# Attention and two mixtures of experts on one core: staggered first blocks, a catch-up after them, and new figures for the host-side scheduler

## The chip, the cores and the metric

One core of a Trainium2 chip runs the whole program in one launch. The metric is the device time of an execution in microseconds, as the median of several runs. Five engines work side by side, each through its own list of instructions in the order in which the program wrote them: TensorE (PE in the rows, its weight loads PEld), VectorE (DVE), ScalarE (ACT), GpSimd (POOL), and SyncE (SP), which here only issues transfers.

## The reference, cut to what matters

```python
def phi(x):                                   # q, k: 4 x 8 x 576 x 64, w_phi: 64 x 128
    proj = np.einsum('bhsd,df->bhsf', x, w_phi)
    proj = proj - np.max(np.abs(proj), axis=-1, keepdims=True)
    return np.concatenate([np.exp(proj), np.exp(-proj)], axis=-1)
q_p, k_p = phi(q), phi(k)
kv = np.einsum('bhsf,bhsd->bhfd', k_p, v)
z = np.sum(k_p, axis=2)
attn = np.einsum('bhsf,bhfd->bhsd', q_p, kv) / (np.einsum('bhsf,bhf->bhs', q_p, z)[..., None] + 1e-06)
x = attn.transpose(0, 2, 1, 3).reshape(2304, 512)
h = x @ moe_w_in                              # 512 x 2048, held as 64-bit floats
x = (h - np.tanh(h)) @ moe_w_out              # 2048 x 512: "first MoE"
p = probs / (probs.sum(-1, keepdims=True) + 1e-09)
out = sum(p[:, e:e + 1] * (np.maximum(x @ w1[e], 0) @ w2[e]) for e in range(4))   # "second MoE"
```

## The kernel before

**Stages.** The attention turns 2304 tokens into x, in 8 blocks of 288 tokens. The first MoE has a hidden width of 2048, cut into 16 chunks of 128. The weights of 8 chunks fit into SBUF at a time (the tiles `wslot`), so the first MoE goes over all tokens twice: in the first pass block j of 288 tokens goes through chunks 0 to 7 as soon as its x exists, while the attention of block j+1 runs between; in the second pass 6 blocks of 384 tokens go through chunks 8 to 15 ("late" in the code), and the two partial sums are added. Then comes the second MoE, which the change doesn't touch.

**Attention.** `k_task(b, p, t0)` makes the features of two heads of k and their product with v (16 of them; 4 ahead of block 0, two more in each of blocks 0 to 5). `q_task(b, s, p, t0)` makes two heads of q for one block (4 a block): transposes, a projection in three matmuls (high and low halves of the operands), copies `pq` and exponentials `ea` and `eb` by ScalarE, a row maximum by VectorE (`qm`, L585), twelve products with `kv` for each of `ea` and `eb` (L598), the division, and a transpose back into `xmem`, which holds x as a high and a low part for two blocks at a time (ring `xt_r`). When a block is done, x is also stored in DRAM (`xs`), for the second pass.

**One visit of a chunk** by a block is `moe_slot` and `moe_x2`. Layer 1 is 12 matmuls of 288 columns (L373, `bank<-xmem,wslot`). Then h - tanh(h) is made: ScalarE squares and takes tanh (L651, L652), VectorE does L653, L654, L655 and the predicated copy L657, ScalarE L656 and the high part `ghm` (L658), and GpSimd or VectorE the low part `glm` (L248 or L247, by the lists `GL` and `GL2`). Layer 2 is 12 matmuls into the four accumulators (`acc`), held back by `LAG = 3` visits. After a block's last visit `evac` copies the accumulators out by ScalarE (L715) and stores them in DRAM (`x2s`).

**Weights.** A chunk has two parts (w_in and w_out). `to_f32` loads one as 64-bit words and makes 32-bit floats by one ScalarE, one GpSimd (L321) and three VectorE instructions (L322, L323, L324); `split_w` makes the high part by ScalarE (L329) and the low part by GpSimd (L330). `direct` does that for chunks 0 to 7. `park` makes the floats of chunks 8 to 15 during blocks 3 to 6 and stores them in DRAM; `staged` loads and splits them when the slots come free, around the start of the second pass.

**Order.** The order of every engine's list comes from a simulation on the host before the launch. `add` puts a piece of work (a node) with an engine, a modelled duration, the nodes it needs and a due time into a graph; `Issue.run` plays the graph through, and each time that an engine falls idle it emits the ready node with the lowest due time. A due time is only a priority: a node that is ready early goes early. `HOP` is the modelled time from the end of a node to a node that waits for it; `c_act`, `c_dve`, `c_pool` and `c_pe` are modelled durations by width. On the chip the order is fixed, and each instruction waits for what it needs. `T_START`, `T_BLK`, `LEAD`, `W_LEAD` and `T_TASK` place the due times: block j's at 50 + 44 j us.

Of the kernel before, what the change touches and what calls it, by code (L numbers as in the profile page):

```python
# [40 lines left out]
class Node:  # L41
    __slots__ = ("eng", "dur", "busy", "fn", "need", "after", "at", "key", "banks", "frees", "home")
# [29 lines left out]
class Issue:  # L72
# [3 lines left out]
    HOP = {"PE": 0.28, "ACT": 0.16, "DVE": 0.16, "POOL": 0.22, "SP": 0.1}  # L76
# [26 lines left out]
    def run(self):  # L103
        ready = {e: [] for e in self.HOP}
        idle = dict.fromkeys(self.HOP, True)
        back = False
        events, n, now = [], 0, 0.0
# [10 lines left out]
        while events:  # L118
# [11 lines left out]
            for e, r in ready.items():  # L130
# [8 lines left out]
                if r:  # L139
# [43 lines left out]
def c_pe(n):  # L183
    return max(n * 0.000417 + 0.013, 0.112)
# [3 lines left out]
def attention_moe_moe_kernel(  # L188
# [122 lines left out]
    def to_f32(c, part, due, early=0.0):  # L311
# [99 lines left out]
    def k_task(b, p, t0):  # L411
# [38 lines left out]
        pd = add("PE", 1.05, proj, [a1], t0 + 1.2, [kT, *kds], banks=pb)  # L450
        for e in range(2):
            bk, kd, kp, due = pb[e], kds[e], kp_r.take(), t0 + 2 + e
# [3 lines left out]
            x1 = add("ACT", c_act(512), lambda kd=kd, kp=kp: ACT.activation(out=kp.t[:, :, 0, :], in_=kd.t, func=ACTF.Exp), [a], due + 1, [kd, kp])  # L456
            x2 = add("ACT", c_act(512), lambda kd=kd, kp=kp: ACT.activation(out=kp.t[:, :, 1, :], in_=kd.t, func=ACTF.Exp, scale=-1.0), [a], due + 1, [kd, kp])
# [19 lines left out]
        for e in range(2 if b else 0):  # L477
# [53 lines left out]
    def q_task(b, s, p, t0):  # L531
# [28 lines left out]
        for e in range(2):  # L560
# [305 lines left out]
    for i in range(2):  # L866
        lx_r.turns.append(xt_r.turns[i - 2])
# [235 lines left out]
```

## Time and profile before

| | |
|---|---|
| median of 3 runs | 1439.3 us |
| lowest and highest | 1436.97 and 1439.79 us |
| profiled execution, its own time | 1439.52 us |
| its span, first to last instruction | 1436.8 us |
| PE busy | 1398.9 us, 97% |
| DVE, ACT, POOL busy | 1067.8, 663.6, 670.8 us |
| mean granted TensorE clock | 0.994 |

The views cover the span; 2.7 us of the execution's own time lie outside it. Ends of matmuls are modelled and matmuls overlap, so PE's busy share is a rough upper bound of its work. The granted clock is a share of full speed (1.00 is 2.4 GHz, half of it 1.2 GHz).

### The profile page before, as it was taken

What the parts mean: (1) busy time and instruction counts of PE and PEld (TensorE: products, weight loads), DVE (VectorE), ACT (ScalarE), POOL (GpSimd) and SP (SyncE); (2) the same over time, 40 slices, a digit from 0 to 9 for tenths busy, and PEclk for the clock granted to TensorE, in tenths of its full rate; (3) what the DMA queues carried; (4) which work ended last, traced back from release to release, by engine and by line L of the source; (5) the groups of instructions that cost most, each with busy time, mean ns of one, the idle gap of its engine ahead of it and who ended that gap; (6) DMA issues with size and microseconds to landing.
All of it is one profiled execution on the core that took longest, in us unless ns stands there. A gap on an engine that the chain in (4) does not pass through costs nothing.

```text
span 1436.8 us, 23312 instructions
## 1 busy us (share of the span) xinstructions
PE 1398.9 (97%) x8704; PEld 1274.5 (89%) x8704; DVE 1067.8 (74%) x1871; ACT 663.6 (46%) x1575; POOL 670.8 (47%) x551
## 2 busy tenths in 40 slices
PE   8988999999999999999899999999999999999998
PEld 6777888989999899998799999898999989999997
DVE  5898578888867867556787777877777787777774
ACT  6756566666656545444433333433333343333331
POOL 2786354554413326213544544654454466445441
PEclk9999999999999999999999999999999999999999
DMA  6532235443416413212212212233122123221211
GB/s 175 166 112 58 83 88 152 131 131 105 136 56 202 120 45 104 62 34 69 85 60 74 68 65 73 68 110 103 65 68 74 59 74 109 67 73 60 74 44 44
DMA packets 128704, 127.43 MB, mean 89 GB/s; under 512 B 53968, under 2 KB 104272, under 8 KB 128592
## 3 DMA queue, kind: packets, MB, share of 16 engines
q1 hardware_dynamic: 128432, 125.89, 28.4%
q8 instruction: 68, 1.11, 0.3%
q14 instruction: 44, 0.36, 0.1%
q10 hardware_dynamic: 160, 0.07, 0.0%
HBM read 101.29 MB, written 24.64 MB: 88 GB/s over the span
## 4 chain that ended last, share of the span: by engine, by line
PE 83%; DVE 8%; ACT 3%; POOL 2%; issue 2%; DMA 1%; SPq 1%; ACTq 0%; DVEq 0%; POOLq 0%
PE acc L373 36%; PE bank L373 35%; PE bank L598 3%; DVE hsm L655 2%; PE bank L498 1%; PE bank L582 1%; DVE thm L657 1%; PE bank L556 1%; DVE glm L247 1%; PE acc L498 1%; PE bank L448 1%; PE acc L508 1%; DVE thm L654 1%; ACT sqm L656 1%; DVE hsm L653 1%
## 5 line engine op out<-in xcount | busy, mean ns | idle before, releaser
L1034 ACT ACTIVATE h<-xc 128x384 fp32r<-128x384 f32 x160 | 84.1, 525 | 426.7 <-DVE xc L1038 426.7
L923 POOL TENSOR_TENSOR wslot<-wtmp,wslot 128x512 fp32r<-128x512 f32 x96 | 124.2, 1294 | 274.2 <-ACT wslot L921 171.6
L373 PE MATMUL acc<-ghm,wslot 128*128 128x288 f32 (+1 forms) x896 | 234.8, 323 | 7.9 <-ACT ghm L658 4.7
L373 PE MATMUL bank<-xmem,wslot 128*128 128x288 f32 (+1 forms) x1224 | 218.3, 314 | 1.8 <-ACT kv L528 1.6
L373 PEld LDWEIGHTS bank<-xmem,wslot 128*128 128x128 f32 x1224 | 187.5, 189 | 3.5 <-ACT kv L528 1.8
L373 PE MATMUL acc<-wslot,h 128*128 128x512 f32 x768 | 188.3, 392 | 0.0
L1010 POOL TENSOR_TENSOR wslot<-raw,wslot 128x512 fp32r<-128x512 f32 x96 | 138.0, 1457 | 100.8 <-ACT wslot L1010 100.8
L1035 DVE SCALAR_TENSOR_TENSOR h<-xc,h 128x384 fp32r<-128x384 f32 x160 | 103.2, 645 | 94.7 <-ACT h L1034 94.7
L373 PEld LDWEIGHTS acc<-ghm,wslot 128*128 128x128 f32 x896 | 159.9, 190 | 14.0 <-ACT ghm L658 5.5
L373 PE MATMUL bank<-wslot,h 128*128 128x512 f32 x672 | 168.2, 395 | 1.5 <-ACT h L1034 1.5
L373 PEld LDWEIGHTS acc<-wslot,h 128*128 128x128 f32 x768 | 143.2, 188 | 27.7
L248 POOL TENSOR_TENSOR glm<-thm,ghm 128x288 fp32r<-128x288 f32 (+1 forms) x76 | 72.9, 960 | 179.3 <-ACT ghm L658 161.5
L373 PEld LDWEIGHTS bank<-wslot,h 128*128 128x128 f32 x672 | 126.0, 189 | 27.1 <-ACT h L1034 2.3
L373 PE MATMUL acc<-glm,wslot 128*128 128x288 f32 (+1 forms) x448 | 141.3, 315 | 3.4 <-POOL glm L248 2.6
L923 POOL TENSOR_TENSOR wslot<-raw,wslot 128x512 fp32r<-128x512 f32 x96 | 108.7, 1152 | 15.6 <-ACT wslot L921 15.6
L657 DVE COPY_PREDICATED thm<-sqm,hsm 128x288 f32<-128x288 int32 (+1 forms) x112 | 77.2, 690 | 43.4 <-ACT sqm L656 43.0
L656 ACT ACTIVATE sqm<-sqm,b_m 128x288 f32<-128x288 f32 (+1 forms) x112 | 64.3, 574 | 87.6 <-DVE hsm L655 85.3
L1038 DVE TENSOR_TENSOR xc<-bank,xc 128x384 f32<-128x384 f32 x168 | 92.3, 550 | 12.1 <-PE bank L373 12.0
L1038 DVE TENSOR_TENSOR xc<-acc,xc 128x384 f32<-128x384 f32 x168 | 92.2, 550 | 11.2 <-PE acc L373 10.9
L919 DVE TENSOR_TENSOR wtmp<-raw 128x256 f32<-128x256 f32 x96 | 98.4, 1026 | 0.0
L653 DVE SCALAR_TENSOR_TENSOR hsm<-bank,sqm 128x288 f32<-128x288 f32 (+1 forms) x110 | 54.6, 496 | 52.3 <-ACT thm L652 51.5
L373 PEld LDWEIGHTS acc<-glm,wslot 128*128 128x128 f32 x448 | 85.2, 190 | 4.8 <-POOL glm L248 3.2
(267 smaller groups left out, 3181.7 us busy)
## 6 DMA issues: line engine op xcount, KB each, us to landing
raw<-in_moe_w_dram SPq DMA_DIRECT2D x96, 512.0 KB, 3.5
xs<-xmem SPq DMA_DIRECT2D x16, 576.0 KB, 4.2
raw<-in_moe_w_in_dram SPq DMA_DIRECT2D x16, 512.0 KB, 4.6
raw<-in_moe_w_out_dram SPq DMA_DIRECT2D x16, 512.0 KB, 5.2
qraw<-in_q_dram SPq DMA_DIRECT2D x32, 144.0 KB, 2.9
x2s<-x2m SPq DMA_DIRECT2D x8, 576.0 KB, 3.4
out_dram<-yacc SPq DMA_DIRECT2D x18, 256.0 KB, 2.1
kraw<-in_k_dram SPq DMA_DIRECT2D x16, 256.0 KB, 3.6
```

What stands on the lines that cost most here:

```text
L248: return add("POOL", c_pool(n), lambda: POOL.tensor_tensor(out=o, in0=a, in1=b, op=op), deps, due, bufs)
L373: PE.matmul(ps, lhsT=a, rhs=b, start=start and n == 1, stop=stop and n == 3 * len(pairs))
L598: PE.matmul(side(ab)[:, e, r], lhsT=x.t[:, e, r * QP:(r + 1) * QP], rhs=kv.t[:, e, ab], start=True, stop=True)
L653: y1 = add("DVE", c_dve(N), lambda: DVE.scalar_tensor_tensor(out=hs.t, in0=at(bk)[:, 0:N], scalar=P1, in1=sq.t, op0=ALU.mult, op1=ALU.mult ...
L656: x3 = add("ACT", c_act(N, ptr=True), lambda: ACT.activation(out=sq.t, in_=sq.t, func=ACTF.Relu, scale=-1.0, bias=b_m[:, 0:1]), [y3], due ...
L657: y4 = add("DVE", c_dve(N), lambda: DVE.copy_predicated(out=th.t, mask=sq.t.bitcast(I32), data=hs.t), [x3, y2, y3], due + 1.4, [th, sq, hs])
L919: steps = [("DVE", 0.36, lambda o=o, a=a, b=b, op=op: DVE.tensor_tensor(out=o, in0=a, in1=b, op=op)) for o, a, b, op in sums]
L923: steps.append(("POOL", c_pool(n), lambda h=h, l=l, src=src: POOL.tensor_tensor(out=l, in0=src, in1=f32(h), op=ALU.subtract)))
L1010: todo2 = [lambda c=c: (ACT.activation(out=vh[:, c], in_=r2[:, c], func=ACTF.Copy), POOL.tensor_tensor(out=vl[:, c], in0=r2[:, c], in1=f32 ...
L1034: ACT.activation(out=hh, in_=src, func=ACTF.Relu)
L1035: DVE.scalar_tensor_tensor(out=hl, in0=src, scalar=0.0, in1=f32(hh), op0=ALU.max, op1=ALU.subtract)
L1038: DVE.tensor_tensor(out=o, in0=bk, in1=a, op=ALU.add)
```

## The change

The first pass no longer takes all 8 chunks through every block: block 0 visits chunks 0 and 1, block 1 chunks 0 to 3, block 2 chunks 0 to 5, and blocks 3 to 7 all eight (`FIRST`). After block 7, three catch-up blocks make the missing 6, 4 and 2 visits: each loads its x again from `xs` into the ring `xt_r` and ends with `add_x2` in place of `evac`, which loads the stored partial sum, adds the four accumulators to it on VectorE and stores it again. Chunk c is asked for by the first block that visits it (`need`). The second pass starts with the ring where the catch-up left it.

The scheduler's model is replaced: durations by width, hops, a drain at the end of a node, a switch time on TensorE when a node has another tile shape (`mode`), and one shared `port` for every GpSimd node and the marked VectorE nodes, which the simulation runs one after the other. Due times get new constants. In `q_task` the exponentials read the copy `pq` in SBUF, two instructions of 2 x 288 columns, instead of the two PSUM banks, four of 288; the 24 products with `kv` become two nodes of 12, one for `ea` and one for `eb`. The projection itself is as it was.

The diff, cut: the scaling of due times inside `k_task` and `q_task` by `K_PACE` and `Q_PACE`, the marks `mode` and `port` on single nodes, and the durations written into single nodes (those of the weights' conversion among them) are left out.

```diff
-T_START = 50.0
+T_START = 44.3
 LEAD = 26.0
-T_BLK = 44.0
-K_LEAD = 0.0
+T_ATT = 22.0
+T_SLOT = 3.3
+T_X2 = 14.8
+K_PACE = 0.78
+Q_PACE = 0.96
+PARK_LEAD = -8.8
+FIRST = (2, 4, 6)
+K_LEAD = -0.4
 GL = ["POOL"]
 GL2 = ["DVE", "POOL"]
-W_LEAD = 5.0
-T_TASK = 8.0
+W_LEAD = 10.5
+T_TASK = 7.7
...
-    HOP = {"PE": 0.28, "ACT": 0.16, "DVE": 0.16, "POOL": 0.22, "SP": 0.1}
+    HOP = {"PE": 0.055, "ACT": 0.037, "DVE": 0.033, "POOL": 0.08, "SP": 0.1}
+    DRAIN = {"PE": 0.16, "ACT": 0.11, "DVE": 0.082, "POOL": 0.035, "SP": 0.0}
+    SWITCH = 0.2
...
-                    event(now + x.busy, "idle", e)
-                    end = now + x.dur
+                    start = now
+                    if x.port:
+                        start = max(now, port)
+                    if e == "PE" and x.mode != mode:
+                        start, mode = now + self.SWITCH, x.mode
+                    event(start + x.busy, "idle", e)
+                    end = start + x.dur + self.DRAIN[e]
+                    if x.port:
+                        port = start + x.busy
...
 def c_act(n, psum=False, ptr=False):
-    return n / 1200.0 + (0.05 if psum else 0.093) + (0.093 if ptr else 0.0)
+    return n * 0.00091 + 0.03 if psum else n * 0.00081 + (0.205 if ptr else 0.105)
 def c_dve(n, fast=False):
-    return n / 960.0 + 0.09
+    return n / 960.0 + 0.066
 def c_pool(n):
-    return n * 0.00225 + 0.22
+    return n * 0.00228 + 0.1
...
-            def exps(e=e):
-                for x, sg in ((ea, 1.0), (eb, -1.0)):
-                    xe.append(add("ACT", c_act(N, True), lambda x=x, sg=sg: ACT.activation(out=x.t[:, e], in_=at(pb[e])[:, 0:N], func=ACTF.Exp, scale=sg), [a], t0 + 2.4, [x], frees=[pb[e]]))
+        xe = [add("ACT", c_act(2 * N), lambda x=x, sg=sg: ACT.activation(out=x.t, in_=pq.t, func=ACTF.Exp, scale=sg), pc, t0 + Q_PACE * 2.4, [pq, x]) for x, sg in ((ea, 1.0), (eb, -1.0))]
...
-        a = add("PE", 2.05, mm, [*xe, s2, *kvdone], t0 + 5, [ea, eb, kv, u], banks=nb)
+        pm = [add("PE", 1.02, lambda ab=ab, x=x: mm(ab, x), [xe[ab], *([] if ab else [s2]), *kvdone], t0 + Q_PACE * 5 + 0.5 * ab, [x, kv, u], bank=nb[ab]) for ab, x in enumerate((ea, eb))]
...
-    t_blk = [T_START + j * T_BLK for j in range(NBLK + 1)]
+    n_first = [FIRST[j] if j < len(FIRST) else NC1 for j in range(NBLK)]
+    t_len = [(T_ATT if j + 1 < NBLK else 0.0) + T_SLOT * n_first[j] for j in range(NBLK)]
+    t_blk = [T_START + sum(t_len[:j]) for j in range(NBLK + 1)]
+    need = [min(j for j in range(NBLK) if n_first[j] > c) for c in range(NC1)]
...
     for c in range(NC1):
-        wdone[c] = direct(c, c, t_blk[0] + W_LEAD * (c - 1))
+        j = need[c]
+        wdone[c] = direct(c, c, t_blk[j] + t_len[j] / n_first[j] * c - W_LEAD * 2)
...
+    def add_x2(j, due):
+        def fn(ends):
+            xb = x2p_r.take()
+            ld = dma([(xb.t, x2s[j])], [x2_done[j]], due - 12, [xb])
+            done = []
+            for i in range(KD):
+                a = add("DVE", c_dve(N), lambda i=i: DVE.tensor_tensor(out=xb.t[:, i, :], in0=accs[i][:, 0:N], in1=xb.t[:, i, :], op=ALU.add), [ends[i], ld], due, [xb])
+                acc_users[i].append(a)
+                done.append(a)
+            x2_done[j] = dma([(x2s[j], xb.t)], done, due + 1, [xb])
+        return fn
...
-        moe_block(j, [(c, c) for c in range(NC1)], xt, xdone, t_blk[j], T_BLK / NC1, GL if j < 4 else GL2 if j < NBLK - 1 else ["DVE"], evac, s_rings, N, LAG)
+        moe_block(j, [(c, c) for c in range(n_first[j])], xt, xdone, t_blk[j], t_len[j] / n_first[j], GL if j < 4 else GL2 if j < NBLK - 1 else ["DVE"], evac, s_rings, N, LAG)
...
-    t2, dt = t_blk[NBLK - 1] + 24, 4.2
+    t2 = t_blk[NBLK]
+    for j in range(len(FIRST)):
+        rest = [(c, c) for c in range(n_first[j], NC1)]
+        xt = xt_r.take()
+        ld = dma([(f32(xt.t[i]), xs[j][i]) for i in range(2)], [xs_done[j]], t2 - 10, [xt])
+        moe_block(j, rest, xt, [ld], t2, T_SLOT, ["DVE", "POOL"], add_x2, s_rings, N, LAG)
+        t2 += T_SLOT * len(rest)
```

## Rows read from the trace of the kernel before

**Rows 1.** The page's first line: the span.

```profile
span 1436.8 us, 23312 instructions
...
```

**Rows 2.** Stretches: length; PE, PEld, DVE, ACT, POOL busy (count); clock; DMA share; GB/s.

```profile
...
0.00:40.00 40.00, 35.49 (x312) 27.82 (x314) 24.48 (x64) 25.04 (x67) 11.50 (x13) 0.96 0.68 173
40.00:60.00 20.00, 19.45 (x199) 15.86 (x195) 14.94 (x32) 13.87 (x40) 13.84 (x10) 1.00 0.55 157
60.00:140.00 80.00, 67.67 (x552) 59.33 (x551) 73.76 (x135) 51.43 (x141) 61.94 (x52) 0.96 0.34 102
140.00:200.00 60.00, 59.67 (x539) 53.11 (x538) 39.00 (x86) 36.98 (x109) 28.74 (x33) 1.00 0.26 75
200.00:420.00 220.00, 217.57 (x1906) 198.67 (x1904) 175.66 (x383) 140.98 (x408) 101.06 (x95) 1.00 0.38 118
420.00:455.00 35.00, 35.00 (x267) 35.00 (x266) 23.56 (x48) 19.84 (x50) 8.86 (x8) 1.00 0.57 173
455.00:480.00 25.00, 21.74 (x129) 20.91 (x129) 22.97 (x33) 18.35 (x43) 15.77 (x11) 0.95 0.59 174
...
655.00:700.00 45.00, 37.91 (x200) 34.35 (x200) 29.50 (x48) 17.99 (x39) 16.29 (x13) 1.00 0.27 88
...
```

**Rows 3.** The same view, the first 20 us of the third stretch.

```profile
...
60.00:80.00 20.00, 18.79 (x186) 16.08 (x184) 18.88 (x41) 14.54 (x43) 15.99 (x15) 1.00 0.51 155
...
```

**Rows 4.** The chain that ended last, from 60 to 140 us, by line.

```profile
...
by line: issue 13.7%; PE bank L373 9.0%; POOL wtmp L321 6.5%; POOL glm L248 6.5%; DVE thm L657 4.8%; POOL wslot L330 4.7%; DVE hsm L655 4.6%; DVE kd L455 4.0%; PE acc L373 3.6%; DVE km L454 3.1%; POOL xf L608 2.9%; POOL ks L485 2.8%; ACT kp
...
```

**Rows 5.** Groups of VectorE instructions from 60 to 140 us: busy, mean ns, idle before.

```profile
...
L324 DVE SCALAR_TENSOR_TENSOR wtmp<-raw,wtmp 128x512 uint32<-128x512 uint32 x10 | 9.8, 993 | 0.0
L655 DVE SCALAR_TENSOR_TENSOR hsm<-sqm,hsm 128x288 f32<-128x288 f32 x10 | 9.3, 928 | 0.0
...
L657 DVE COPY_PREDICATED thm<-sqm,hsm 128x288 f32<-128x288 int32 x10 | 8.1, 824 | 0.3 <-ACT sqm L656 0.3
...
```

**Rows 6.** Groups of VectorE instructions from 200 to 420 us, same columns.

```profile
...
L657 DVE COPY_PREDICATED thm<-sqm,hsm 128x288 f32<-128x288 int32 x35 | 21.2, 606 | 7.6 <-ACT sqm L656 7.2
L655 DVE SCALAR_TENSOR_TENSOR hsm<-sqm,hsm 128x288 f32<-128x288 f32 x34 | 20.1, 591 | 0.0
L585 DVE TENSOR_REDUCE qm<-bank 96x3 f32<-96x384 f32 x36 | 19.0, 548 | 11.9 <-PE bank L582 9.2 <-ACT eb L566 2.4 <-ACT x2m L715 0.2
L653 DVE SCALAR_TENSOR_TENSOR hsm<-bank,sqm 128x288 f32<-128x288 f32 x34 | 15.4, 452 | 11.5 <-ACT thm L652 10.9
L654 DVE TENSOR_TENSOR thm<-bank,thm 128x288 f32<-128x288 f32 x34 | 15.2, 446 | 0.0
L323 DVE SCALAR_TENSOR_TENSOR wtmp<-raw,wtmp 128x512 uint32<-128x512 uint32 x16 | 14.3, 895 | 0.2
L324 DVE SCALAR_TENSOR_TENSOR wtmp<-raw,wtmp 128x512 uint32<-128x512 uint32 x16 | 14.0, 877 | 0.0
...
L322 DVE TENSOR_SCALAR wtmp<-wtmp 128x512 uint32<-128x512 uint32 x16 | 9.0, 565 | 4.2 <-POOL wtmp L321 4.2
...
L454 DVE TENSOR_REDUCE km<-bank 128x4 f32<-128x512 f32 x12 | 7.7, 682 | 1.6 <-PE bank L448 1.6
...
```

**Rows 7.** VectorE in order of time, 440 to 482 us: start, length, instruction.

```profile
...
441.08 0.45 DVE L655 SCALAR_TENSOR_TENSOR hsm<-sqm,hsm 128x288 f32<-128x288 f32 x1
...
444.25 1.40 DVE L655 SCALAR_TENSOR_TENSOR hsm<-sqm,hsm 128x288 f32<-128x288 f32 x1
...
```

**Rows 8.** GpSimd in order of time, 440 to 480 us, same columns.

```profile
...
444.05 2.77 POOL L330 TENSOR_TENSOR wslot<-raw,wslot 128x512 fp32r<-128x512 f32 x2 [9.24 <-ACT wslot L329]
...
```

**Rows 9.** Waits from 440 to 500 us: in total, times, longest.

```profile
...
PE acc L373 <- ACT x2m L715: 3.2, 1, 3.2
...
```

**Rows 10.** DMA issues by transfer: count, KB each, median us from issue to landing.

```profile
...
xmem<-xs SPq DMA_DIRECT2D x4, 576.0 KB, 4.3
...
```

**Rows 11.** Groups of ScalarE instructions from 140 to 440 us: busy, mean ns, idle before.

```profile
...
L566 ACT ACTIVATE eb<-bank 128x288 f32<-128x288 f32 x44 | 19.6, 445 | 0.0
...
L456 ACT ACTIVATE kp<-kd 128x512 f32<-128x512 f32 x18 | 11.3, 629 | 6.5 <-DVE kd L455 5.2 <-POOL wtmp L321 1.2
...
```

More of the change, by code (lines that the diff above doesn't have):

```diff
@@ L41 @@
 class Node:
-    __slots__ = ("eng", "dur", "busy", "fn", "need", "after", "at", "key", "banks", "frees", "home")
+    __slots__ = ("eng", "dur", "busy", "fn", "need", "after", "at", "key", "banks", "frees", "home", "mode", "port")
 class Bank:
@@ L81, in __init__, with add @@
         self.free_lent, self.n_lent = list(range(banks, banks + lent)), lent
-    def add(self, eng, dur, fn, deps=(), due=0.0, bufs=(), bank=None, banks=(), frees=(), busy=None, early=0.0, home=False):
+    def add(self, eng, dur, fn, deps=(), due=0.0, bufs=(), bank=None, banks=(), frees=(), busy=None, early=0.0, home=False, mode="all", port=False):
         x = Node()
-        x.home = home
+        x.home, x.mode, x.port = home, mode, port or eng == "POOL"
         x.eng, x.dur, x.busy, x.fn, x.banks, x.key = eng, dur, busy or dur, fn, [bank] if bank else list(banks), (due, len(self.nodes))
@@ L106, in run @@
         back = False
+        mode, port = "all", 0.0
         events, n, now = [], 0, 0.0
@@ L246, in tt @@
         if eng == "DVE":
-            return add("DVE", c_dve(n), lambda: DVE.tensor_tensor(out=o, in0=a, in1=b, op=op), deps, due, bufs)
+            return add("DVE", c_dve(n), lambda: DVE.tensor_tensor(out=o, in0=a, in1=b, op=op), deps, due, bufs, port=True)
         return add("POOL", c_pool(n), lambda: POOL.tensor_tensor(out=o, in0=a, in1=b, op=op), deps, due, bufs)
@@ L448, in proj @@
                     PE.matmul(at(pb[e])[:, j * 128:(j + 1) * 128], lhsT=kT.t[h0:h0 + 64, j * 128:(j + 1) * 128], rhs=wphi[h0:h0 + 64, :], start=True, stop=True)
-        pd = add("PE", 1.05, proj, [a1], t0 + 1.2, [kT, *kds], banks=pb)
+        pd = add("PE", 0.9, proj, [a1], t0 + K_PACE * 1.2, [kT, *kds], banks=pb, mode="rows")
         for e in range(2):
-            bk, kd, kp, due = pb[e], kds[e], kp_r.take(), t0 + 2 + e
+            bk, kd, kp, due = pb[e], kds[e], kp_r.take(), t0 + K_PACE * (2 + e)
             m = km.t[:, 4 * e:4 * e + 4]
@@ L625, in to_p @@
             return t[:, p, :].rearrange("d (p r) -> d p r", r=3)
-        a = add("ACT", c_act(N, True), lambda: ACT.activation(out=to_p(xh), in_=from_r(), func=ACTF.Copy), [a], due + 2.5, [xt], frees=[ob])
+        a = add("ACT", c_act(N, True), lambda: ACT.activation(out=to_p(xh), in_=from_r(), func=ACTF.Copy), [a], due + Q_PACE * 2.5, [xt], frees=[ob])
         done.append(a)
-        a = add("DVE", c_dve(N), lambda: DVE.tensor_tensor(out=to_p(xl), in0=from_r(), in1=to_p(f32(xh)), op=ALU.subtract), [a], due + 3, [xt], frees=[ob])
+        a = add("DVE", c_dve(N), lambda: DVE.tensor_tensor(out=to_p(xl), in0=from_r(), in1=to_p(f32(xh)), op=ALU.subtract), [a], due + Q_PACE * 3, [xt], frees=[ob])
         done.append(a)
         if p == NP - 1:
-            xs_done[j] = dma([(xs[j][i], f32(xt.t[i])) for i in range(2)], done, due + 3, [xt])
+            xs_done[j] = dma([(xs[j][i], f32(xt.t[i])) for i in range(2)], done, due + Q_PACE * 3, [xt])
         n_att[0] += 1
@@ L828, in fn @@
             def fn(order, s=s, c=c, gg=gg, first=first, last=last, due=due):
-                ends = moe_x2(s, wdone[c], gg, first, last, due + lag * dt, order, n)
+                ends = moe_x2(s, wdone[c], gg, first, last, due + T_X2, order, n)
                 if last:
-                    end(j, due + lag * dt + 1)(ends)
+                    end(j, due + T_X2 + 1)(ends)
                 return ends
@@ L863, in x_again @@
                 SP.dma_start(out=f32(t)[:, :, o:o + m], in_=src[:, k0:k0 + n, a:a + m])
-    lx_r = Ring([lambda i=i: late_xt(i) for i in range(2)])
-    for i in range(2):
-        lx_r.turns.append(xt_r.turns[i - 2])
+    xt_first = len(xt_r.turns) % 2
+    lx_r = Ring([lambda i=i: late_xt((i + xt_first) % 2) for i in range(2)])
+    lx_r.turns.extend(xt_r.turns[-2:])
     l_rings = []
```

109 lines of the change are left out of this document (52 added, 57 removed).

## The prediction

> **What bounds the kernel now.** I read the span cut into stretches first, then the chain of waits in the worst stretch, then the groups of VectorE instructions there and in a good stretch. The change leaves alone everything after the second pass of the first MoE, and there PE hardly stops. PE's lost time lies earlier. I count as lost the time without a matmul, plus length times (1 - clock) where the granted clock's mean is under 1.00. From 0 to 60 us that is 4.5 + 0.6 idle and 0.04 x 40 = 1.6 of clock, 6.7 us. From 60 to 140 us it is 80 - 67.67 = 12.3 idle and 0.04 x 80 = 3.2 of clock: 15.5 us, the largest sum. From 140 to 200 it is 0.3, from 200 to 420 2.4, from 455 to 480 3.3 + 0.05 x 25 = 4.5, from 655 to 700 7.1 [rows 2]. So the pass that the change rebuilds holds some 29 us to be had at the very most, 2% of a span of 1436.8 us [rows 1].
>
> In the worst stretch VectorE is busy 73.76 of 80 us (92%) and GpSimd 61.94 (77%); from 200 to 420 us they are at 80% and 46% [rows 2]. The chain there runs through both of them and matmuls are a small part of it [rows 4]. The reader sees why in the counts: ten of the 16 weight parts that the first visits need (L324 x10) and ten visits (L655 x10) fall into these 80 us [rows 5]. Block 0 asks for all eight chunks' weights at once, and PE has no other work ready.
>
> **Prices.** A visit on PE is 24 of the 267 matmuls that fill 35 us [rows 2], 3.15 us. From 200 to 420 us there are 34 visits (L655), 18 q tasks (two L585 each) and 6 k tasks (two L454 each) [rows 6]; PE's 217.57 us less 34 x 3.15 leave 110.5 us, 4.6 a task, so 27.6 for a block's six tasks. On VectorE a visit is 0.606 + 0.591 + 0.452 + 0.446 = 2.10 us, a part 0.895 + 0.877 + 0.565 = 2.34 us [rows 6]; the remainder of 175.66 - 71.9 - 37.3, less some 6 us of smaller groups, is 60 us or 2.5 a task, 15 a block. In the worst stretch the visit's L655 and L657 are 0.34 and 0.22 us dearer and the part's L324 0.12 [rows 5, 6]: 2.65 a visit, and 2.45 a part.
>
> **The first blocks.** Before, block 0 with the ten parts costs VectorE 15 + 8 x 2.65 + 10 x 2.45 = 60.7 us against 27.6 + 8 x 3.15 = 52.8 on PE: VectorE is the bound by 8 us, and waits on chains make it 15.5. After, I spread these ten parts over blocks 0 to 2 as 4, 4 and 2, though due times are only priorities. VectorE then has 15 + 5.3 + 9.8 = 30.1 us beside 33.9 on PE, 15 + 10.6 + 9.8 = 35.4 beside 40.2, and 15 + 15.9 + 4.9 = 35.8 beside 46.5: 89, 88 and 77%. I don't believe the third, as the parts slip, and take 88% for it too. What PE loses at such a share I interpolate: 1.1% at 80% (2.4 of 220 us [rows 2]) and 6.0% at 94% (60 to 80 us: 1.21 of 20 [rows 3]), so 4% at 88 or 89%: 4.8 us over the 120.6 us. The term is -15.5 - 0.3 + 4.8 = -11 us. Its ends are -15.8 (no loss left) and 0: at the whole worst stretch's rate, 15.5 in 80 us at 92%, 120 us would lose 23 us and nothing is won.
>
> The Trainium skill, "Perfetto Trace Analysis", section "Identifying the Most-Contended Engine", says that the share of matmul time is a poor measure of TensorE and that weight-load time is a better one. By it the worst stretch has 59.33 of 80 us of weight loads, 74%, against 90.3% from 200 to 420 us [rows 2], which is 12.9 us of loads missing, or 14.3 us of time; the term would be -9.8 instead of -11. The trace agrees with the rule in kind, and I keep my count.
>
> **The catch-up.** The 12 visits move; PE's 12 x 3.15 = 37.8 us stay the same and now stand where no attention runs. There VectorE is at 23.56 of 35 us [rows 2], 2.1 us a visit by its share. Added are 12 additions of an accumulator to SBUF, priced by L654, which also has one operand in each memory: 0.446 us [rows 6], 5.4 us, so 2.1 + 0.45 = 2.6 us beside 3.15 on PE, 81%: hidden but for about 1% of 37.8 us, and if the cover is gone, 5.4 us. The loads of x (two per block, 4.3 us to landing [rows 10]) are covered by 6 and 4 visits for the first two blocks. The second pass's first load must wait until the second catch-up block has left its buffer; PE then has two layers 1 and three layers 2 left, 5 x 1.6 = 8 us, against 4.3 to 8.6 us for one transfer or two in turn: 0 to 1 us. The 6 loads of x, 3 loads and 3 stores of sums also pass SP's queue among the parked weights; its transfers keep the DMA engines 38 to 59% busy here [rows 2]. I take +1 us, between 0 and +18 (below).
>
> **The scheduler's figures** change the order everywhere ahead of the second MoE, and the trace of before can't show the new order. What they can win lies in the losses outside the worst stretch: 6.7 us from 0 to 60, 2.4 from 200 to 420, and 4.5 from 455 to 480, 13.6 us; the wait for transfers in the first 20 us stays. What they can lose is not bounded by a row; I take the same size as the nearest comparable, 4.5 us, for another bad stretch. I choose -2.5, nearer to nothing than to the gain.
>
> **The query tasks.** Four exponentials from PSUM at 0.445 us become two from SBUF of 576 columns, 0.71 us each by L456's 0.629 for 512 [rows 11]: 1.78 us become 1.42 per task on ScalarE, which is 64% busy [rows 2]. The first twelve products wait for one exponential less. Other tasks and visits hide both; with no cover it would be at most the 2.4 us counted above. The split of the 24 products adds no matmul. All this: 0.
>
> **Sum.** -11 + 1 - 2.5 = -12.5 us from the profiled execution's own 1439.5 (2.7 over its span), 0.2 above the median of the runs, so 1426.8 against 1439.3: I predict 1427 us. A change under 0.2% (2.9 us) can't be told from none.
>
> **Rivals.** *More is won*: the new figures fit well enough that the first blocks lose only 1.1%, as from 200 to 420 us (1.3 us), and two thirds of the other 13.6 us go too: -14.5 - 9 + 1 = -22.5, 1417 us. For it: L655 and L657 take 0.93 and 0.82 us in the worst stretch and 0.59 and 0.61 in the good one [rows 5, 6], and the old model has one duration for each; against: some of the 6.7 us at the start is waiting for transfers.
>
> *It doesn't do what it says*: the same parts and tasks ahead of block 3 keep VectorE and GpSimd at 92%, and the loss only spreads. The first term is 0 to -3, the rest as above: 1438 us. For it: the part work isn't less, it only comes later; against: PE now has other blocks' attention to run meanwhile.
>
> *The catch-up becomes VectorE's and GpSimd's* (slower). The second pass's weights are split by GpSimd just there; beside two such splits, 2.77 us [rows 8], L655 took 1.40 us instead of 0.45 [rows 7]. With 0.95 more on each visit, VectorE needs 2.6 + 0.95 = 3.55 us against 3.15: 12 x 0.4 = 4.8 us behind. Each of three more block ends then hands the accumulators over late, as PE waited 3.2 us for L715 once [rows 9]: 9.6 us; and the late load adds up to 4. That is 18 us, net of the gains of -13.5 a time of 1444 us. It decides once the catch-up loses over 16 us. The Trainium skill, "SBUF — State Buffer", section "Who interferes with whom", states that a VectorE instruction with two SBUF operands and a GpSimd one that reads SBUF shut each other out for a whole instruction; by that rule L655 and L657 of every catch-up visit beside a split are held, as the rows on L655 agree, while the additions are not.
>
> **Chances and range.** Forecast 0.54 (own range 1420 to 1433), more won 0.22, not what it says 0.12, slower 0.12. Faster by over 0.2%: the first two and a sixth of the third, 0.78; same 0.1; slower 0.12. The range 1411 to 1441 reaches from the second's better end to the foot of the fourth.
>
> **What would show it.** Right: from 60 to 140 us PE idle under 6 us with the clock at 1.00, VectorE under 92%; the second pass beginning some 12 us earlier than before's 455; no wait of over 2 us on the accumulators between the catch-up blocks. Wrong: VectorE over 95% in the catch-up, PE waiting on additions or on `xmem`, or the loss found again between 140 and 300 us. What would break the forecast most is the order itself, which no row shows.

## The result, and the profile after

The changed kernel takes 1421.4 us (median of four runs, 1418.5 to 1425.1) beside 1438.6 for the kernel before on the same chip: a ratio of 0.9883 with an interval of 0.9855 to 0.991. That is 5.6 us below the forecast of 1427, in the range and in the forecast's own range of 1420 to 1433, but 4.4 us above the rival "more is won" (1417), so nearer to that as a time; as a change, -17.1 us lies between the -12.5 of the one and the -22.5 of the other. The profiled execution took 1419.9 us. Its span:

```profile
span 1417.9 us, 23306 instructions
...
```

The matmuls are the same 8704 in both. The stretches of the span, up to 200 us as in [rows 2] and from there cut 15 to 20 us earlier, to stand at the same work (columns as there):

```profile
...
0.00:40.00 40.00, 34.35 (x295) 27.41 (x295) 24.78 (x60) 25.30 (x59) 15.29 (x17) 0.96 0.70 187
40.00:60.00 20.00, 19.72 (x202) 15.30 (x203) 19.26 (x38) 16.41 (x44) 11.40 (x10) 1.00 0.51 147
60.00:140.00 80.00, 76.84 (x720) 66.47 (x719) 68.70 (x144) 55.71 (x148) 59.64 (x53) 0.98 0.42 122
140.00:200.00 60.00, 56.45 (x496) 50.19 (x496) 47.56 (x99) 37.72 (x100) 36.30 (x37) 0.97 0.41 129
200.00:400.00 200.00, 197.53 (x1695) 182.47 (x1692) 157.93 (x349) 128.05 (x340) 80.05 (x77) 1.00 0.37 119
400.00:440.00 40.00, 40.00 (x303) 40.00 (x303) 30.02 (x61) 25.44 (x63) 14.66 (x12) 1.00 0.46 157
440.00:465.00 25.00, 25.00 (x171) 25.00 (x171) 21.79 (x40) 16.15 (x36) 11.70 (x9) 1.00 0.82 269
465.00:640.00 175.00, 175.00 (x1011) 174.91 (x1010) 126.78 (x216) 87.41 (x179) 52.13 (x43) 1.00 0.25 74
640.00:680.00 40.00, 34.93 (x192) 32.76 (x190) 26.61 (x41) 15.50 (x32) 17.08 (x13) 1.00 0.28 87
...
```

Lost time, counted as in the prediction:

| part of the work (before / after) | before | after |
|---|---|---|
| start, 0 to 60 us | 6.7 | 7.5 |
| first blocks, 60 to 140 | 15.5 | 4.8 |
| 140 to 200 | 0.3 | 5.3 |
| 200 to 420 / 200 to 400 | 2.4 | 2.5 |
| handover to the second pass, 420 to 480 / 400 to 465 | 4.5 | 0 |
| second pass, 480 to 655 / 465 to 640 | 1.7 | 0 |
| its end, 655 to 700 / 640 to 680 | 7.1 | 5.1 |
| sum | 38.2 | 25.2 |

So 13.0 of the 18.9 us by which the span is shorter are lost time that is gone, against a forecast of 12.5. The other 5.9 us are nearly all busy time of the same matmuls (1398.9 to 1392.3 us, 6.6 less, of which the table has counted 1.1 as clock), and the prediction left them out. Where they lie is seen at equal work, by the start of the n-th matmul in each trace (the stretches above are cut by time, and count less):

| up to matmul | after is ahead by, us | won since the line above | by the table above |
|---|---|---|---|
| 3800, the second pass has begun | 6.7 | 6.7 | 4.8 |
| 3900, behind the stall at the handover | 12.0 | 5.3 | 4.5 |
| 4500, in the second pass | 13.9 | 1.9 | 1.7 |
| 5200, behind its end | 17.0 | 3.1 | 2.0 |
| the last | 19.1 | 2.1 | not counted |

So all but the last line is won where lost time is won too. The 2.1 us of the last line come in the second MoE, which the change leaves alone: the granted clock is 0.91 from 980 to 1000 us before and 1.00 from 960 to 980 us after, at about the same work. In e7 below nothing is won there (17.6 us ahead at matmul 5200, 17.4 at the end), so I put these 2.1 us down to the execution and not to the change.

In the worst stretch the chain of waits now runs mostly through PE itself, where [rows 4] had GpSimd's L321 and L248 near its head:

```profile
...
by line: PE bank L600 15.4%; PE acc L389 10.5%; PE bank L514 8.9%; PE acc L600 5.2%; PE bank L389 4.2%; PE bank L572 3.8%; DVE wtmp L339 3.5%; DVE wtmp L340 3.3%; PE bank L585 2.9%; PE acc L514 2.9%; PE bank L464 2.9%; issue 2.6%; PE bank L
...
```

The groups of VectorE instructions there, to hold against [rows 5] (L340 was L324, L657 was L655, L659 was L657; busy, mean ns, idle before):

```profile
...
L340 DVE SCALAR_TENSOR_TENSOR wtmp<-raw,wtmp 128x512 uint32<-128x512 uint32 x8 | 6.9, 867 | 0.0
...
L657 DVE SCALAR_TENSOR_TENSOR hsm<-sqm,hsm 128x288 f32<-128x288 f32 x5 | 3.1, 612 | 0.0
L659 DVE COPY_PREDICATED thm<-sqm,hsm 128x288 f32<-128x288 int32 x5 | 2.8, 553 | 0.0
...
```

Ten visits have become five and ten parts eight, and a visit's two long instructions are a third shorter (928 and 824 ns before). PE filled the time with other blocks' attention: its count rose from 552 to 720. But 140 to 200 us, nearly full before, now loses 5.3 us with VectorE at 79%, not 65%. Over both stretches 5.7 us are saved, not 11.

These stretches are cut by time, not by work. The start of the second pass is in keeping with them: its first product comes 5.6 us ahead of before's 455 (PE in order of time):

```profile
...
449.40 1.41 PE L389 MATMUL bank<-xmem,wslot 128*128 128x384 f32 x7
...
```

### The profile page after: what moved, and what is told of

It reads as the page before. It is cut to its first block, busy times and chain, and to the rows that moved or that the text cites. A ratio compares the mean times of both kernels' runs of the same rounds, so it can differ in the third digit from the quotient of the medians.

```text
span 1417.9 us, 23306 instructions
## 1 busy us (share of the span) xinstructions
PE 1392.3 (98%) x8704; PEld 1272.5 (90%) x8704; DVE 1075.4 (76%) x1889; ACT 664.9 (47%) x1511; POOL 660.9 (47%) x545
## 4 chain that ended last, share of the span: by engine, by line
PE 90%; DVE 5%; ACT 2%; DMA 2%; issue 1%; SPq 0%; POOL 0%; ACTq 0%; DVEq 0%
PE acc L389 39%; PE bank L389 38%; PE bank L600 3%; PE bank L514 2%; PE bank L585 1%; PE bank L572 1%; PE acc L600 1%; DVE hsm L657 1%; PE bank L464 1%; DVE xc L1063 1%; PE acc L514 0%; DMA raw<-in_moe_w_out_dram 0%; DMA xq<-x2f 0%; PE bank L528 0%; PE bank L615 0%
## 5 line engine op out<-in xcount | busy, mean ns | idle before, releaser
L389 PE MATMUL acc<-ghm,wslot 128*128 128x288 f32 (+1 forms) x896 | 231.1, 320 | 0.0
L264 POOL TENSOR_TENSOR glm<-thm,ghm 128x288 fp32r<-128x288 f32 (+1 forms) x70 | 66.7, 953 | 188.4 <-ACT ghm L660 174.9
L659 DVE COPY_PREDICATED thm<-sqm,hsm 128x288 f32<-128x288 int32 (+1 forms) x112 | 80.0, 714 | 37.2 <-ACT sqm L658 36.8
L1063 DVE TENSOR_TENSOR xc<-bank,xc 128x384 f32<-128x384 f32 x168 | 92.2, 549 | 11.7 <-PE bank L389 11.7
L1063 DVE TENSOR_TENSOR xc<-acc,xc 128x384 f32<-128x384 f32 x168 | 92.2, 550 | 11.2 <-PE acc L389 10.9
L655 DVE SCALAR_TENSOR_TENSOR hsm<-bank,sqm 128x288 f32<-128x288 f32 (+1 forms) x110 | 54.5, 496 | 44.4 <-ACT thm L654 43.6
```

The lines of the kernel that those rows point to most:

```text
L264: return add("POOL", c_pool(n), lambda: POOL.tensor_tensor(out=o, in0=a, in1=b, op=op), deps, due, bufs)
L389: PE.matmul(ps, lhsT=a, rhs=b, start=start and n == 1, stop=stop and n == 3 * len(pairs))
L655: y1 = add("DVE", c_dve(N), lambda: DVE.scalar_tensor_tensor(out=hs.t, in0=at(bk)[:, 0:N], scalar=P1, in1=sq.t, op0=ALU.mult, op1=ALU.mult ...
L659: y4 = add("DVE", c_dve(N), lambda: DVE.copy_predicated(out=th.t, mask=sq.t.bitcast(I32), data=hs.t), [x3, y2, y3], due + 1.4, [th, sq, hs ...
L1063: DVE.tensor_tensor(out=o, in0=bk, in1=a, op=ALU.add)
```

## The experiments

Each kernel is "after" or "before" with one edit. Ratios are to the kernel before on the same chip.

**e1: the change without the stagger.** All due times and figures of after, but every block goes through 8 chunks.

```diff
-FIRST = (2, 4, 6)
+FIRST = ()
```

> The changed kernel with FIRST = (): all blocks make eight visits, no catch-up; the scheduler's figures, due times and query tasks stay changed. Theory A (taking visits and weight parts out of block 0 is most of the gain, as the prediction's first term has it, 11 of 17 us): about 1432 us, with PE's loss from 60 to 140 us back near 15 us. Rival B (the scheduler's figures are most of it): 1424 us or less, the loss from 60 to 140 us under 8 us.

Measured: 1449.5 us, 1.0084 (1.0058 to 1.0111). Both theories missed. The new constants without the stagger are 10 us slower than before. Two stretches of e1, and a wait from 60 to 140 us:

```profile
...
60.00:140.00 80.00, 58.51 (x464) 51.22 (x464) 69.17 (x116) 43.84 (x109) 55.07 (x49) 0.85 0.29 85
...
440.00:500.00 60.00, 60.00 (x415) 60.00 (x414) 46.79 (x91) 39.06 (x92) 25.12 (x18) 1.00 0.57 178
...
```

```profile
...
PEld bank L389 <- ACT wslot L345: 10.6, 1, 10.6
...
```

From 60 to 140 us PE loses 21.5 + 0.15 x 80 = 33.5 us. Its weight loads stand in one wait for 10.6 us, for the high part of a weight that ScalarE makes: a layer 1 comes in PE's list before its weights can be there, and all that is behind it waits too. From here to after are 28 us, so the stagger and the constants can't be added up from "before". The second pass begins at 473 us here, and PE is full from 440 to 500 us: the handover has no stall, though there is no catch-up.

**e2 and e3: after with the old figures, and after with the old query tasks.** e2 takes the old hops and the old durations by width and of the weights' conversion, and no drain, switch or port; the due times stay new. e3 takes back the four exponentials from PSUM and the one node of 24 products.

```diff
-    HOP = {"PE": 0.055, "ACT": 0.037, "DVE": 0.033, "POOL": 0.08, "SP": 0.1}
-    DRAIN = {"PE": 0.16, "ACT": 0.11, "DVE": 0.082, "POOL": 0.035, "SP": 0.0}
-    SWITCH = 0.2
+    HOP = {"PE": 0.28, "ACT": 0.16, "DVE": 0.16, "POOL": 0.22, "SP": 0.1}
+    DRAIN = {"PE": 0.0, "ACT": 0.0, "DVE": 0.0, "POOL": 0.0, "SP": 0.0}
+    SWITCH = 0.0
...
```

> The changed kernel with the scheduler's old figures for hops, drains, widths and the weights' conversion, and without the shared port and the tile switch; the stagger, the due times and the query tasks stay changed. Theory A: about 1426 us, within 5 us of the changed kernel. Rival B: 1432 us or more, with stalls of 3 to 5 us back where the second pass begins.

> The changed kernel with the old query tasks: four exponentials from PSUM and one node of 24 products. The prediction has 0 for this edit: 1421 us within 3. A rival that it frees PSUM banks earlier and so carries part of the gain: 1426 us or more.

Measured: e2 1432.6 us, 0.9962 (0.9943 to 0.998). Next to the new due times the figures are worth some 11 us. In e2's stretches the first blocks lose 7.6 + 3.2 us and the middle of the first pass 5.9 + 2.0, where after loses 4.8 and 2.5:

```profile
...
60.00:140.00 80.00, 72.44 (x646) 61.13 (x647) 73.37 (x135) 57.25 (x150) 62.67 (x55) 0.96 0.44 134
...
200.00:400.00 200.00, 194.11 (x1667) 178.55 (x1666) 157.21 (x341) 123.62 (x325) 88.67 (x83) 0.99 0.38 121
...
```

Rival B's number holds (1432 or more), but not its stall: PE is busy for all of the 40 us from 440 us on.

e3 takes 1424.7 us, 0.9903 (0.9882 to 0.9925), an interval that overlaps after's: the query tasks can't be told from nothing. In its stretches it loses 5.6 + 1.6, 4.7 + 3.6 and 1.2 us, where after loses 4.8, 5.3 and 2.5:

```profile
...
60.00:140.00 80.00, 74.43 (x673) 63.11 (x671) 70.94 (x137) 56.90 (x164) 58.97 (x53) 0.98 0.42 120
140.00:200.00 60.00, 55.27 (x475) 47.45 (x474) 44.52 (x94) 36.85 (x106) 32.37 (x32) 0.94 0.39 124
200.00:400.00 200.00, 198.81 (x1724) 183.32 (x1723) 150.62 (x348) 127.09 (x366) 86.20 (x82) 1.00 0.37 117
...
```

**e4: before with the stagger alone.** Before's figures, due times and query tasks; the catch-up and `add_x2` as in after.

```diff
+T_ATT = 22.0
+T_SLOT = 2.75
+FIRST = (2, 4, 6)
...
-    t_blk = [T_START + j * T_BLK for j in range(NBLK + 1)]
+    n_first = [FIRST[j] if j < len(FIRST) else NC1 for j in range(NBLK)]
+    t_len = [T_ATT + T_SLOT * n_first[j] for j in range(NBLK)]
+    t_blk = [T_START + sum(t_len[:j]) for j in range(NBLK + 1)]
...
```

> The kernel before with the stagger and the catch-up alone, its own figures, query tasks and constants (a block is 22 + 2.75 us a visit, which is the old 44 at eight visits). Theory A: about 1428 us. Rival B: 1436 us or more, as the order that the old figures make loses elsewhere what the stagger wins.

Measured: 1426.1 us, 0.9912 (0.9892 to 0.9931). The stagger alone has most of the gain. Its stretches:

```profile
...
60.00:140.00 80.00, 72.03 (x650) 61.45 (x651) 72.97 (x141) 56.59 (x164) 62.97 (x56) 0.96 0.42 124
140.00:200.00 60.00, 57.77 (x520) 51.58 (x519) 45.47 (x101) 40.01 (x116) 36.02 (x36) 1.00 0.44 136
...
440.00:480.00 40.00, 40.00 (x258) 39.98 (x257) 30.75 (x64) 22.55 (x49) 13.58 (x11) 1.00 0.74 228
...
465.00:640.00 175.00, 173.32 (x1001) 173.00 (x1000) 115.85 (x204) 85.08 (x175) 53.74 (x44) 1.00 0.26 75
...
```

From 60 to 140 us it loses 8.0 + 0.04 x 80 = 11.2 us, and 2.2 from 140 to 200: 13.4 where before loses 15.8. The handover is full, as in after, without the new figures. From 465 to 640 us it loses 1.7 as before does, which after doesn't.

**e5, e6 and e11: without the conversion on VectorE.** e5 is before and e6 is after without L322 to L324 for chunks 0 to 7; e11 is e5 without GpSimd's L321 as well.

```diff
-    def to_f32(c, part, due, early=0.0):
+    def to_f32(c, part, due, early=0.0, bits=True):
...
-        a = add("DVE", 0.65, lambda: DVE.tensor_scalar(out=t, in0=t, scalar1=5, scalar2=2, op0=ALU.logical_shift_left, op1=ALU.logical_shift_right), [a], due + 1, [tb])
+        a = add("DVE", 0.65, lambda: bits and DVE.tensor_scalar(out=t, in0=t, scalar1=5, scalar2=2, op0=ALU.logical_shift_left, op1=ALU.logical_shift_right), [a], due + 1, [tb])
...
-            src, tb, a = to_f32(c, part, due)
+            src, tb, a = to_f32(c, part, due, bits=False)
```

> The kernel before, with the three VectorE instructions of the weights' conversion (L322, L323, L324) left out for chunks 0 to 7, so these weights are not the right ones; every node stays in the scheduler's plan, so the order is the same. If VectorE's load in block 0 is what holds PE from 60 to 140 us (theory A's first term): PE's idle time there falls from 12.3 us to under 6, and the time by 6 to 12 us. Rival C (GpSimd's L321 and L330 with the wait chain through them hold it, and VectorE is only blocked by them): idle stays over 9 us, the time within 4 us of before.

> The changed kernel with the same three VectorE instructions left out for chunks 0 to 7. PE still loses time from 140 to 200 us in the changed kernel (3.6 us idle and clock under 1.00), which theory A takes for conversions that slipped there: then that loss goes and the time falls by 4 to 8 us. Rival: the loss is the price of the order or of GpSimd's locks, and the time falls by less than 3 us.

> The kernel before, with GpSimd's L321 and VectorE's L322, L323 and L324 left out for chunks 0 to 7, so these weights are not the right ones; the plan is the same. Leaving out VectorE's three alone left 7.9 us of idle PE from 60 to 140 us. If GpSimd's share of the conversion holds the rest: idle under 4 us and the time 4 us or more below the 1431 us of that run. If the rest is waits along the order's chains: idle still over 6 us and the time within 2 us of it.

Measured: e5 1431.1 us, 0.9947 (0.9932 to 0.9961); e6 1417.9 us, 0.9855 (0.984 to 0.9869), which overlaps after; e11 1430.6 us, 0.995 (0.9931 to 0.9969). One row of e5, two of e6, one of e11:

```profile
...
60.00:140.00 80.00, 72.07 (x619) 63.42 (x621) 57.24 (x119) 54.18 (x149) 57.59 (x55) 0.98 0.33 98
...
```

```profile
...
60.00:140.00 80.00, 78.32 (x751) 68.33 (x750) 56.97 (x126) 58.71 (x155) 54.83 (x55) 1.00 0.46 135
140.00:200.00 60.00, 57.13 (x486) 49.81 (x484) 44.18 (x93) 35.63 (x93) 33.85 (x35) 0.94 0.38 115
...
```

```profile
...
60.00:140.00 80.00, 73.17 (x626) 64.15 (x625) 56.35 (x118) 54.28 (x149) 46.01 (x47) 0.98 0.34 100
...
```

With VectorE down to 57 of 80 us, before's worst stretch still loses 7.9 + 1.6 = 9.5 of its 15.5 us, and with GpSimd down to 46 too it still loses 8.4. The time of e5 falls by 7.5 us, as theory A had it, but PE's idle time only to 7.9 us; e11 comes out as the second case of its expectation, waits along the order's chains. So the conversion on VectorE was rather less than half of that loss; the load that VectorE keeps, of visits and attention, was not varied. What is left in e11 is nine waits of PE for seven different tiles, made by ScalarE, VectorE and GpSimd, the longest 1.7 us for `ghm` and 1.6 for `kv`. In e6 1.7 us are lost from 60 to 140 us instead of after's 4.8, and the loss from 140 to 200 us stays: 2.9 idle and 0.06 x 60 of clock.

**e7 and e8: less and more stagger.** 6 visits moved, or 17, instead of 12.

```diff
-FIRST = (2, 4, 6)
+FIRST = (4, 6)
```

```diff
-FIRST = (2, 4, 6)
+FIRST = (2, 3, 4, 6)
```

> The changed kernel with FIRST = (4, 6): 6 visits are moved instead of 12. Theory A, with the gain in proportion to the visits taken out of the first blocks: halfway between the changed kernel and the one without stagger, 1433 to 1438 us. Rival D (the gain comes from having any catch-up between block 7 and the second pass): within 4 us of the changed kernel, 1421 to 1425.

> The changed kernel with FIRST = (2, 3, 4, 6): 17 visits are moved instead of 12, in four catch-up blocks. Theory A: the load of blocks 1 to 3 falls further, where PE still loses 5 us, so 1414 to 1419 us. Rival: the catch-up begins to cost, or PE runs out of work beside the attention, and the time is 1421 us or more.

Measured: e7 1421.5 us, 0.9875 (0.9858 to 0.9891); e8 1422.8 us, 0.9888 (0.9873 to 0.9903). Neither can be told from after. Half of the visits moved already gives the whole gain, so it isn't proportional to the relief. In e7 the handover is full too:

```profile
...
440.00:480.00 40.00, 40.00 (x258) 40.00 (x257) 34.17 (x68) 24.59 (x56) 13.91 (x11) 1.00 0.72 231
...
```

**e9: after with half of the low parts on VectorE.** `GL` gives every second `glm` of blocks 0 to 3 to VectorE, to relieve GpSimd at 140 to 200 us.

```diff
-GL = ["POOL"]
+GL = ["DVE", "POOL"]
```

> The changed kernel with the low parts of blocks 0 to 3 made by VectorE and GpSimd in turn instead of GpSimd alone. In the changed kernel one L657 lasted 3.9 us at 158 us beside GpSimd instructions that followed each other without a gap, and PE waited 2.7 us. If GpSimd's load is what PE still loses to from 140 to 200 us: 3 us or more gained, 1418 us or less. Rival: VectorE is as full there, and the time is the same or up to 4 us more.

Measured: 1423.0 us, 0.9883 (0.9862 to 0.9904). No gain; from 140 to 200 us PE is busy 55.88 us, with VectorE at 50.74 instead of 47.56. So `glm` on GpSimd alone isn't what holds PE there.

**e10: before with block 7's copy-out on VectorE.** This tests whether the handover stalled behind ScalarE's queue ([rows 9]).

```diff
+                if j == NBLK - 1:
+                    a = add("DVE", c_dve(N), lambda i=i: DVE.tensor_copy(out=xb.t[:, i, :], in_=accs[i][:, 0:N]), [ends[i]], due, [xb])
+                else:
```

> The kernel before, with block 7's accumulators copied out by VectorE instead of ScalarE, and nothing else. In the profile of before the copies L715 stand in ScalarE's list behind L656, which waits for VectorE's L655, held by GpSimd's splits. Theory E (that queue is the stall where the second pass begins): PE's wait of 3.2 us and the lower clock after it go, 1433 to 1435 us. Rival: VectorE, busy 92% of that stretch, copies out as late, and the time is within 2 us of before.

Measured: 1441.9 us, 1.0017 (1.0005 to 1.0028), no gain. The wait stays and changes its name (waits from 440 to 500 us: in total, times, longest):

```profile
...
PE acc L373 <- DVE x2m L716: 4.8, 1, 4.8
...
```

**e12: before with a late catch-up only.** Blocks 0 and 1 go through all 8 chunks, so the start isn't relieved; block 2 takes 2, and its 6 others are caught up after block 7.

```diff
+FIRST = (8, 8, 2)
...
+        if not rest:
+            continue
```

> The kernel before with FIRST = (8, 8, 2) and its own figures: block 0 makes all eight visits and asks for all weights, as before; only block 2 leaves six visits to one catch-up block after block 7, so weight slots come free earlier and the second pass's splits can spread. Theory H (the stall where the second pass begins is crowding of GpSimd's splits, and any catch-up spreads them): idle PE from 60 to 140 us stays near 12 us, the stall of 3 to 5 us at the start of the second pass goes, 1433 to 1435 us. Rival (relief of block 0 is needed for the gain there too): 1438 us or more.

Measured: 1445.0 us, 1.0044 (1.0027 to 1.0062). The rival's number (1438 or more) holds, but not its reason, since the rows separate the two effects:

```profile
...
60.00:140.00 80.00, 67.97 (x552) 59.09 (x551) 73.09 (x136) 51.37 (x141) 62.59 (x52) 0.96 0.33 102
...
200.00:250.00 50.00, 44.87 (x379) 39.27 (x379) 37.80 (x82) 30.45 (x89) 21.23 (x22) 0.93 0.47 142
...
440.00:480.00 40.00, 39.97 (x287) 39.62 (x286) 29.71 (x61) 26.72 (x65) 16.63 (x14) 1.00 0.55 167
...
```

From 60 to 140 us it loses as much as before, and yet the handover is full (before: 21.74 of 25 us, [rows 2]). The time is lost from 200 to 250 us: 5.1 + 0.07 x 50 = 8.6 us, where before loses 1.3. I take this to be PE without work, since block 2's visits are missing there; no run tests it.

## Why the prediction was right, and where it wasn't

**The first blocks** are the step that was mis-sized: -11 forecast, -5.7 measured from 60 to 200 us. What failed is "What PE loses at such a share I interpolate". Read from the trace after, VectorE at 86% went with 6.0% of PE lost (4.8 of 80 us), and VectorE at 79% with 8.8% (5.3 of 60): the share doesn't set the loss. The prediction's own rows say so already: 94% from 60 to 80 us went with 6.0%, and 92% over the whole 80 us with 19% (15.5 us). e11 shows it from the other side: VectorE at 70% and GpSimd at 58%, and 10.5% lost. The relief itself came as described, five visits fewer and PE filled with other blocks' attention; then, as the rival "it doesn't do what it says" had it, part of the loss moved into the next stretch. The range named for this term, -15.8 to 0, holds the value. At equal work the whole pass up to the second one gives 6.7 us.

One wait of 140 to 200 us can be followed. PE waits for `ql` (waits from 140 to 200 us):

```profile
...
PE bank L572 <- DVE ql L562: 2.7, 1, 2.7
...
```

and VectorE made `ql` late because L657 ahead of it took 3.88 us instead of 0.43 (VectorE in order of time: start, length):

```profile
...
158.05 3.88 DVE L657 SCALAR_TENSOR_TENSOR hsm<-sqm,hsm 128x288 f32<-128x288 f32 x1
161.85 0.45 DVE L562 TENSOR_TENSOR ql<-bank,qh 128x288 fp32r<-128x288 f32 x1
...
163.32 0.43 DVE L657 SCALAR_TENSOR_TENSOR hsm<-sqm,hsm 128x288 f32<-128x288 f32 x1
...
```

Meanwhile GpSimd, same columns:

```profile
...
157.71 0.73 POOL L501 TENSOR_TENSOR ks<-ks,kpr 64x256 f32<-64x256 f32 x1
158.41 1.31 POOL L498 TENSOR_TENSOR tz<-kp 128x512 f32<-128x512 f32 x1
159.67 1.26 POOL L346 TENSOR_TENSOR wslot<-wtmp,wslot 128x512 fp32r<-128x512 f32 x1
160.89 0.72 POOL L504 TENSOR_TENSOR ks<-tz 128x256 f32<-128x256 f32 x1
164.17 0.80 POOL L264 TENSOR_TENSOR glm<-thm,ghm 128x288 fp32r<-128x288 f32 x1 [2.56 <-ACT ghm L660]
```

This accounts for 2.7 of 3.6 us idle; the next waits are 0.6 us for `xmem` and 0.2 for `glm`. The other 1.8 us are clock, and they follow the wait (after in steps of 5 us; nothing is under 1.00 elsewhere from 140 to 200 us):

```profile
...
160.00:165.00 5.00, 2.65 (x18) 2.45 (x19) 4.21 (x7) 2.98 (x8) 2.41 (x3) 0.90 0.27 91
165.00:170.00 5.00, 5.00 (x43) 4.56 (x44) 3.19 (x9) 2.15 (x7) 3.27 (x4) 0.76 0.43 127
...
```

VectorE's conversions are not the cause: in e6 PE waits for `ql` just so. Nor does this one wait hold the time by itself: in e9 it is gone, and PE waits 4.0 us for four other results. The longest of each, from 140 to 200 us, e6 first:

```profile
...
PE bank L572 <- DVE ql L562: 2.3, 1, 2.3
...
PE bank L600 <- ACT kT L451: 1.2, 1, 1.2
...
```

**The handover** was a term of 4.5 us that the prediction gave to the scheduler's figures, as something that they might win. It went, and there are two ways to that on record. The catch-up does it with the old figures: e4 and e12 (no relief at the start) have no stall there. The new figures and due times do it without a catch-up: e1 has none either, and at equal work it wins 5.0 us on before over the same 100 matmuls (3800 to 3900), as after wins 5.3. So the prediction's reading is not refuted, and which of the two counts in after isn't known. Before, all 16 of GpSimd's weight splits there came in the 36 us after 444 us, beside the first products of the second pass; this is its group from 440 to 480 us:

```profile
...
L330 POOL TENSOR_TENSOR wslot<-raw,wslot 128x512 fp32r<-128x512 f32 x16 | 23.0, 1463 | 22.6 <-ACT wslot L329 22.6
```

After, a part of the visits stands behind the attention, slots come free one by one, and the splits stand spread through the catch-up (GpSimd from 385 to 480 us):

```profile
...
400.90 5.95 POOL L346 TENSOR_TENSOR wslot<-raw,wslot 128x512 fp32r<-128x512 f32 x4 [9.80 <-ACT wslot L345]
...
463.95 2.86 POOL L346 TENSOR_TENSOR wslot<-raw,wslot 128x512 fp32r<-128x512 f32 x2 [0.92 <-ACT wslot L345]
```

This spread is not what it takes: in e1 all 16 splits fall into the 28 us from 463 us, more crowded than in the kernel before, the last eight without a gap (GpSimd from 400 to 500 us), and PE still doesn't wait.

```profile
...
479.45 11.87 POOL L346 TENSOR_TENSOR wslot<-raw,wslot 128x512 fp32r<-128x512 f32 x8 [3.72 <-ACT wslot L345]
```

Nor does e10 decide on ScalarE's queue: on VectorE the copies come no earlier, and PE waits 4.8 us instead of 3.2. What removes the stall stays open.

**The catch-up** cost nothing; +1 was forecast. PE is full from 400 to 465 us, VectorE at 75% and then 87%, and nothing waits on an accumulator or on `xmem` on PE. VectorE from 400 to 465 us, and the loads of x (count, KB, us from issue to landing):

```profile
...
L657 DVE SCALAR_TENSOR_TENSOR hsm<-sqm,hsm 128x288 f32<-128x288 f32 x16 | 10.5, 654 | 0.0
...
L783 DVE TENSOR_TENSOR x2m<-acc,x2m 128x288 f32<-128x288 f32 x10 | 4.1, 451 | 0.4 <-PE acc L389 0.3
...
```

```profile
...
xmem<-xs SPq DMA_DIRECT2D x10, 576.0 KB, 4.5
...
```

An addition takes 0.451 us, against 0.446 by L654, and the load 4.5 us against 4.3. The slower rival's mechanism is there, since single L657 beside a split take up to 1.54 us, but its price isn't: over these 16 visits of 288 columns the mean is 0.654 us, against 0.591 in [rows 6], and not 0.95 more. The cover held. By the rule of the Trainium skill, "SBUF — State Buffer", section "Who interferes with whom", the additions, with one operand in PSUM, should not be held; the trace agrees: all twelve take 0.44 to 0.46 us, those beside the splits at 464 us too.

**The scheduler's figures** were -2.5. From e4 to after it is 4.7 us (1426.1 to 1421.4), but the intervals overlap, and this holds the due times and the query tasks as well. At equal work the two are level until the handover is over (e4 is 6.5 us ahead of before at matmul 3800 and 11.9 at 3900, after 6.7 and 12.0); then e4 stays at 11.9 and 11.7 while after reaches 13.9 and 17.0. A part of it can be seen: the 1.7 us that before and e4 lose in the second pass is gone. This is that stretch of before, and its wait on PE:

```profile
...
480.00:655.00 175.00, 173.32 (x997) 173.00 (x997) 113.18 (x204) 83.90 (x172) 52.94 (x44) 1.00 0.22 65
...
```

```profile
...
PE acc L373 <- POOL glm L248: 1.7, 1, 1.7
...
```

Against old figures with new due times it is 11 us (e2), and the constants without the stagger cost 10 (e1). So there is no one number for the figures, which seem fitted to one order; along the way from e4 to after the record can't tell -2.5 from -4.7.

**The query tasks**, 0 forecast, can't be told from 0 (e3). Their exponentials take 0.687 us for 576 columns, 0.71 estimated (ScalarE from 140 to 440 us):

```profile
...
L576 ACT ACTIVATE eb<-pq 128x576 f32<-128x576 f32 x18 | 12.4, 687 | 0.0
...
```

**The signs.** Of those named for "right", VectorE under 92% (86%), PE idle under 6 us (3.2) and no wait on the accumulators came true; the clock reached 0.98, not 1.00, and the second pass starts 5.6 us earlier, not 12. Of those named for "wrong", the loss between 140 and 300 us came in part. The total came nearer than its terms, and that was luck: the first blocks gave 5.3 us less than forecast, and the handover, the second pass and its end gave 4.5 + 1.7 + 2.0 = 8.2 where 2.5 was put down and of which only the handover was named.

**Open.** Why half of the visits moved give the whole gain (e7), what removes the stall at the handover, and why after gains 2 to 3 us at the end of the second pass, which e4 doesn't.

## What to carry to other kernels

When a stage loses time beside a loaded engine, find the waits before pricing the relief by that engine's share: here taking the conversion off VectorE and GpSimd left half of the loss. Work moved out of a crowded stage should be looked at where it lands too. Before a stall's end is credited to one part of a change, look at the runs that lack that part: here the handover is full with the catch-up and the old figures, and with the new figures and no catch-up. Figures of a planner can be fitted to one order, so test them with and without the new order, from both sides, and don't add the parts.

## What the runs showed of the hardware

A VectorE instruction with both operands in SBUF can be held through several GpSimd instructions. L657 at 158.05 us took 3.88 us while GpSimd ran the rest of L501 and then L498, L346 and L504 without a gap (0.73, 1.31, 1.26 and 0.72 us); it ended at 161.9 us, just after GpSimd fell idle at 160.89 + 0.72 = 161.6 us. In e6 and e7 it happens again: an L657 that starts during L498 takes 3.47 and 3.56 us, and L346 and L504 go first. The prediction had priced such a hold from rows beside splits at 0.95 us more a visit. The section of the Trainium skill named above says that the order of issue decides who blocks. The trace agrees that one engine waits for the other, but by its record L657 starts ahead of L498, L346 and L504 and yet all three go first; here the measurement decides, with the limit that spans on GpSimd are rough.
